# Late heads on SP's queue: a head's store and load of turned probabilities, then the loads of values, queries and keys

## The chip, the cores and the metric

The kernel runs on one core of a Trainium2 chip. The metric is the device time in microseconds (us) of one launch, the median of several runs.

## The reference

Causal attention with a forget gate (4 batches of 8 heads, 576 positions, head size 64) is followed by two dense layers with different activations. Cut to what is computed:

```python
scores = scale * np.matmul(q, k.transpose(0, 1, 3, 2))
cum = np.cumsum(np.log(np.clip(f, 0.0001, 1.0)), axis=-1)
scores = np.where(causal, -1e9, scores + cum[..., :, None] - cum[..., None, :])
attn = np.exp(scores - max); attn = attn / (sum + 1e-09)
x = np.matmul(attn, v)                      # 2304 tokens x 512
h = np.maximum(x @ w_in, 0.0);  x = (h * h) @ w_out        # first layer, d_ff 2048
h = x @ w_in2;                  y = (h - np.tanh(h)) @ w_out2   # second layer
```

## The kernel before

The 32 heads go through attention one by one, while TensorE also works on the first dense layer for tokens whose attention is ready (blocks of 288 tokens, matmuls into hp and yp, L143 and L169). Heads 0 to 15 transpose their probabilities on TensorE. Heads 16 to 31, the late heads, do it in another way, and the change touches these alone:

- scores(k): five tiles of queries, t = 4, 3, 2, 1, 0. TensorE multiplies QA and QB (L490, L491), DVE takes the row minimum out of PSUM into a tile T (L451), ScalarE takes the exponential (L456), and DVE (t = 4, 2, 0) or POOL (t = 3, 1) normalises (L465).
- turn(k, t): DVE transposes each tile in T by blocks of 32 x 32 (L517).
- put_get(k): SP issues five stores of T to a buffer in HBM (p_d, L526 and L527), and after they have landed six loads back into T with the blocks exchanged (L532 and L534).
- split_p(k): POOL makes the high part PTh from T (L95, four instructions), DVE the low part PTl (L106, four).
- pv(k): TensorE multiplies PTh and PTl with the values (o_ps, L576, L570, L573). For an odd head a store of the result follows (x_d, L440 and L441).

There are two tiles T, one for even and one for odd heads (T_191 and T_192 in the rows of the instruction order). PTh and PTl exist once. A head's inputs come by load(u), which fetches queries and keys into R (576 KB, one buffer) and the gate's rows into QB (18 KB, two buffers), and load_v(u), which fetches values into VR (160 KB, two buffers). prep(u) makes QA and QB out of R on ScalarE, DVE and POOL. All these DMAs are issued by SP, in the order of its queue: an instruction that waits holds all that stand behind it.

attention_late() writes the steps of head k and of head k - 1 in turns, in five pieces for each k. From the third block of the dense layer on, which holds nearly all of the late heads, the order on each engine is not the order of this code. A scheduler makes it at build time from the dependencies and its own estimates, so an added tie can move instructions on every engine.

Of the kernel before, what the change touches and what calls it, by code (L numbers as in the profile page):

```python
# [18 lines left out]
NU = B * H  # L19
# [14 lines left out]
UT = 16  # L34
# [24 lines left out]
def kernel(  # L59
# [25 lines left out]
    def pre(u):  # L85
        return "" if u < UT else "l_"

    def by(name):
        return {"A": nc.scalar, "V": nc.vector, "P": nc.gpsimd, "S": nc.sync}[ENG[name]]

    def rounded(eng, out, in_):
        if eng is nc.scalar:
            eng.activation(out, in_, AF.Copy)  # L93
        elif eng is nc.gpsimd:
            eng.tensor_scalar(out, in_, 1.0, 1.0, ALU.mult, ALU.mult)  # L95
        else:
            eng.tensor_copy(out, in_)
# [85 lines left out]
    def latest(engine):  # L183
        return next(x for x in reversed(nc.cur_bb.bb.instructions) if x.engine == engine)
# [43 lines left out]
    def load(u):  # L228
        R[u] = one.tile([128, 2, S], F32, tag="R", name="R")
        nc.sync.dma_start(R[u], qk[u])  # L230
        QB[u] = two.tile([68, 2, S], F32R, tag="QB", name="QB")
        nc.sync.dma_start(QB[u][64:68].bitcast(F32), aug_d[u])
# [15 lines left out]
    def load_v(u):  # L248
        VR[u] = two.tile([128, 5, D], F32, tag="VR", bufs=2, name="VR")
        nc.sync.dma_start(VR[u], v[u])  # L250
# [183 lines left out]
    def store_x(b, pair, xs, c0, c1):  # L434
        STORED.add((b, pair, c1))
        n = c1 - c0
        xh = one.tile([128, S], F32R, tag="xsh", name="xsh")
        rounded(by(pre(b * H) + "xh"), xh[:, :n], xs[:, c0:c1])
        rest(by(pre(b * H) + "xl"), xs[:, c0:c1], xs[:, c0:c1], xh[:, :n])
        nc.sync.dma_start(x_d[b][pair][:, 0, c0:c1], xh[:, :n].bitcast(F32))  # L440
        nc.sync.dma_start(x_d[b][pair][:, 1, c0:c1], xs[:, c0:c1])  # L441
# [25 lines left out]
    def bank(u, name):  # L467
        return psa.tile([128, 512], F32, tag="at", name=name)

    def blocks(u):  # L470
        return PT[u % 2].rearrange("p (k s j) -> p k s j", s=4, j=32)
# [10 lines left out]
    def scores(u, t):  # L482
        qa, qb, st = QA[u], QB[u], ST[u]
        n, q0 = NKEY[t], Q0[t]
        rows = 64 if t == 0 else 128
        cuts = [(0, 320), (320, 576)] if t == 4 else [(0, n)]
        mn = None
        for i, (a, b) in enumerate(cuts):
            ps = bank(u, "s_ps")
            nc.tensor.matmul(ps[:, :b - a], qa[:, 0, q0:q0 + 128], qa[:, 1, a:b], start=True, stop=False)  # L490
            nc.tensor.matmul(ps[:, :b - a], qb[:, 0, q0:q0 + 128], qb[:, 1, a:b], start=False, stop=True)  # L491
            mn = row_min(prob(u, t, a, b), ps, st, t, i, a, b, mn)
        soften(prob(u, t, 0, n), st, t, mn, f"{pre(u)}n{t}")
# [29 lines left out]
    def put_get(u):  # L523
        T, (d, e) = PT[u % 2], p_d[u % 2]
        for q in range(4):
            by("put").dma_start(d.rearrange("(i q) n -> q i n", q=4)[q], T[32 * q:32 * q + 32, :2048])  # L526
        by("put").dma_start(e, T[:, 2048:])  # L527
        src = d.rearrange("(i q) (a b n) -> b i (q a) n", q=4, a=4, b=4)
        end = e.rearrange("(q i) (b s n) -> b i q s n", q=4, b=2, s=2)
        for b in range(4):  # L530
            dst = T[32 * b:32 * b + 32]
            by("get").dma_start(dst[:, :2048].rearrange("p (q n) -> p q n", q=16), src[b])  # L532
            if b < 2:
                by("get").dma_start(dst[:, 2048:].rearrange("p (q n) -> p q n", q=4), end[b][:, :, 1])  # L534
# [9 lines left out]
    def late_pt(k):  # L544
        return PT[k].rearrange("p c j -> p (c j)")[:, :1664].rearrange("p (q c j) -> p q c j", q=4, j=32)

    def pv(u):
        vh, vr = VH.pop(u), VR.pop(u)
        b, h = divmod(u, H)
        e = h % 2  # L550
        ps = bank(u, "o_ps")
        if u < UT:
            hi, lo = (PT[k] for k in "hl")
            po = ps.rearrange("p (s j) -> p s j", s=4)
            at = lambda p, c, t: p[:, 10 - 4 * c + t:14 - 4 * c]
            po4, p4 = ps[0:64, 384:512].rearrange("p (q j) -> p q j", q=4), blocks(0)[0:64, 12:16, 1]
            po_at = lambda t: po[:, t:]
            p0 = blocks(0)[0:64, 8:10, 0]
        else:
            hi, lo = (late_pt(k) for k in "hl")  # L560
            po = ps.rearrange("p (q s j) -> p q s j", q=4, s=4)
            at = lambda p, c, t: p[:, :, CHUNK_AT[c]:CHUNK_AT[c] + 4 - t]
            end = PT[u % 2][0:64, 2048:].rearrange("p (q s j) -> p q s j", q=4, s=2)
            po4, p4 = po[0:64, :, 3], end[:, :, 1]
            po_at = lambda t: po[:, :, t:]
            p0 = end[:, 0:2, 0]
        seq = [(hi, 0), (None, 4), (None, 0), (hi, 1), (lo, 1), (hi, 2), (lo, 2), (hi, 3), (lo, 3), (lo, 0)]
        for n, (pt, c) in enumerate(seq):
            if c == 4:
                nc.tensor.matmul(po4, vr[0:64, 4], p4, start=False, stop=False)  # L570
            elif pt is None:
                ps0 = bank(u, "o0_ps")
                nc.tensor.matmul(ps0[0:64, 0:64], vr[0:64, 0], p0, start=True, stop=True)  # L573
            else:
                t = max(0, c - 1)
                nc.tensor.matmul(po_at(t), vh[:, c].rearrange("p a d -> p (a d)"), at(pt, c, t), start=(n == 0), stop=(n == 9))  # L576
        if e == 0:
            XS[0] = two.tile([128, S], F32, tag="xs", name="xs")
        xs = XS[0]
        r = slice(64 * e, 64 * e + 64)  # L580
        xt = one.tile([64, 512], F32, tag="xsh", name="xt")
        rounded(nc.scalar, xt, ps[64:128])
        if u < UT:
            nc.vector.tensor_tensor(xs[r, 64:], ps[0:64], xt, ALU.add)
        else:
            nc.vector.tensor_tensor(
                xs[r, 64:].rearrange("p (s q j) -> p q s j", s=4, q=4),
                ps[0:64].rearrange("p (q s j) -> p q s j", q=4, s=4),
                xt.rearrange("p (q s j) -> p q s j", q=4, s=4), ALU.add,
            )  # L590
        rounded(by(pre(u) + "xs0"), xs[r, 0:64], ps0[0:64, 0:64])
        if e == 1:
            store_x(b, h // 2, xs, 0, S)
# [11 lines left out]
    def attention(u0):  # L605
        for p in range(u0 - 2, UT):
            if u0 - 1 <= p:
                load_v(p + 1)
            for t in (1, 4, 3, 2):
                if p >= u0:  # L610
                    trans(p, t)
                    yield
                if u0 <= p + 1:
                    scores(p + 1, t)
                    if t == 1:
                        scores(p + 1, 0)
                    elif p + 1 == UT:
                        turn(UT, t)
                    yield
                if t == 4 and p + 2 < NU:  # L620
                    prep(p + 2)
                if t == 3 and p >= u0:
                    prep_v(p)
            if p + 3 < NU:
                load(p + 3)
            if p >= u0:
                pv(p)
            if p + 1 == UT:
                turn(UT, 1)
                turn(UT, 0)  # L630
                put_get(UT)
            if p >= u0:
                yield

    def attention_late():
        for k in range(UT + 1, NU + 1):
            now = k < NU
            if now:
                load_v(k)
                clear(k)  # L640
                scores(k, 4)
            yield
            if now:
                scores(k, 3)
                turn(k, 4)
            yield
            if k + 1 < NU:
                prep(k + 1)
            prep_v(k - 1)
            split_p(k - 1, 0)  # L650
            if now:
                scores(k, 2)
                turn(k, 3)
            yield
            if k + 2 < NU:
                load(k + 2)
            split_p(k - 1, 1)
            if now:
                scores(k, 1)
                scores(k, 0)  # L660
                turn(k, 2)
            yield
            if now:
                turn(k, 1)
                turn(k, 0)
                put_get(k)
            pv(k - 1)
            yield

    X = {0: [f1.tile([128, NK, TB], F32R, tag="xhl", bufs=4, name="xhl") for _ in range(2)]}  # L670
# [223 lines left out]
```

## Time and profile before

| | |
|---|---|
| median of 3 runs | 1102.18 us (1101.27 to 1104.58) |
| profiled execution | 1104.67 us, span 1102.8 us |
| PE busy | 1032.4 us, 94% of the span |
| DVE, ACT, POOL busy | 585.9, 526.7, 255.0 us |
| mean granted TensorE clock | 0.97 |

The share of PE is an average over stages: after some 575 us the attention is over and PE is busy all the time, so the stretch ahead of that is where an order of transfers could matter.

### The profile page before, as it was taken

What the parts mean: (1) busy time and instruction counts of PE and PEld (TensorE: products, weight loads), DVE (VectorE), ACT (ScalarE), POOL (GpSimd) and SP (SyncE); (2) the same over time, 40 slices, a digit from 0 to 9 for tenths busy, and PEclk for the clock granted to TensorE, in tenths of its full rate; (3) what the DMA queues carried; (4) which work ended last, traced back from release to release, by engine and by line L of the source; (5) the groups of instructions that cost most, each with busy time, mean ns of one, the idle gap of its engine ahead of it and who ended that gap; (6) DMA issues with size and microseconds to landing.
All of it is one profiled execution on the core that took longest, in us unless ns stands there. A gap on an engine that the chain in (4) does not pass through costs nothing.

```text
span 1102.8 us, 17026 instructions
## 1 busy us (share of the span) xinstructions
PE 1032.4 (94%) x6048; PEld 909.0 (82%) x6048; DVE 585.9 (53%) x1550; ACT 526.7 (48%) x1221; POOL 255.0 (23%) x374
## 2 busy tenths in 40 slices
PE   4899999998989789989799999999999999999998
PEld 3576779887978688879789999888888888888898
DVE  5886777776677666957533545644222222222222
ACT  6977777764554454645435757532222222222222
POOL 4244455555345353533310000000000000000000
PEclk9989999998998898999899999999999999999999
DMA  7556643228766758766738149300300200110010
GB/s 243 193 148 196 183 154 121 79 79 234 213 172 181 208 146 257 222 145 176 197 84 328 53 143 345 133 1 1 115 1 1 88 27 1 39 39 1 1 39 20
DMA packets 95558, 137.99 MB, mean 125 GB/s; under 512 B 12048, under 2 KB 72016, under 8 KB 93424
## 3 DMA queue, kind: packets, MB, share of 16 engines
q1 hardware_dynamic: 95472, 136.89, 41.4%
q8 instruction: 48, 0.79, 0.3%
q14 instruction: 38, 0.31, 0.1%
HBM read 94.99 MB, written 41.88 MB: 124 GB/s over the span
## 4 chain that ended last, share of the span: by engine, by line
PE 51%; DMA 9%; DVE 4%; SPq 4%; POOL 1%; issue 1%; ACT 1%; POOLq 0%; ACTq 0%; DVEq 0%
PE yp L169 25%; PE hp L143 24%; DMA p_d<-T 4%; DMA T<-p_d 3%; DVE PTl L106 1%; SPq L532 1%; SPq L526 1%; PE o_ps L576 1%; SPq L534 1%; POOL PTh L95 1%; DMA xhl<-x_d 1%; DMA raw<-in_w_dram 1%; DVE T L517 1%; DVE gl L106 1%; DVE T L465 0%
## 5 line engine op out<-in xcount | busy, mean ns | idle before, releaser
L143 PE MATMUL hp<-xhl,w 128*128 128x288 f32 (+2 forms) x2496 | 457.5, 331 | 6.7 <-ACT tmp L153 4.0
L143 PEld LDWEIGHTS hp<-xhl,w 128*128 128x128 f32 x2496 | 394.6, 194 | 45.5 <-ACT tmp L153 5.2
L169 PE MATMUL yp<-ghl,w 128*128 128x512 f32 (+1 forms) x960 | 214.9, 373 | 0.0
L169 PE MATMUL yp<-gh,w 128*128 128x288 f32 x1024 | 199.3, 301 | 0.0
L169 PEld LDWEIGHTS yp<-ghl,w 128*128 128x128 f32 x960 | 167.8, 188 | 34.2
L169 PEld LDWEIGHTS yp<-gh,w 128*128 128x128 f32 x1024 | 161.6, 192 | 1.6 <-issue 0.4
L158 DVE TENSOR_TENSOR tmp<-hp,tmp 128x512 f32<-128x512 f32 (+1 forms) x80 | 51.0, 638 | 208.2 <-ACT tmp L157 208.1
L157 ACT ACTIVATE tmp<-hp 128x512 f32<-128x512 f32 (+1 forms) x80 | 44.5, 556 | 223.2 <-PE hp L143 223.1
L169 PE MATMUL yp<-gl,w 128*128 128x288 f32 x512 | 132.7, 303 | 4.6 <-DVE gl L106 3.7
L153 ACT ACTIVATE tmp<-hp 128x288 f32<-128x288 f32 x128 | 51.7, 405 | 123.3 <-PE hp L143 121.7
L456 ACT ACTIVATE T<-T,ST 128x320 f32<-128x320 f32 (+4 forms) x152 | 82.8, 546 | 45.8 <-DVE ST L451 39.4
L169 PEld LDWEIGHTS yp<-gl,w 128*128 128x128 f32 x512 | 91.0, 193 | 7.2 <-DVE gl L106 5.1
L106 DVE TENSOR_TENSOR gl<-tmp,gh 128x288 fp32r<-128x288 f32 x96 | 47.8, 499 | 64.5 <-ACT tmp L155 63.9
L106 DVE TENSOR_TENSOR PTl<-T,PTh 128x512 fp32r<-128x512 f32 (+1 forms) x64 | 53.0, 857 | 50.0 <-POOL PTh L95 49.0
L106 DVE TENSOR_TENSOR ghl<-tmp,ghl 128x512 fp32r<-128x512 f32 (+1 forms) x80 | 51.1, 639 | 49.1 <-ACT ghl L93 43.8
L451 DVE CUSTOM_DVE_ANT_0 T<-s_ps,mk 128x320 f32<-128x320 f32 (+3 forms) x152 | 61.8, 421 | 21.4 <-PE s_ps L491 13.2
L465 POOL TENSOR_SCALAR T<-T,ST 128x448 f32<-128x448 f32 (+4 forms) x80 | 52.4, 657 | 89.6 <-DVE ST L460 43.3
L93 ACT ACTIVATE ghl<-tmp 128x512 fp32r<-128x512 f32 (+1 forms) x80 | 47.2, 590 | 49.9 <-DVE tmp L158 49.8
L576 PE MATMUL o_ps<-PTh,VH 128*128 128x512 f32 (+1 forms) x96 | 40.4, 421 | 29.3 <-POOL PTh L95 25.4
L95 POOL TENSOR_SCALAR PTh<-T 128x512 fp32r<-128x512 f32 (+1 forms) x64 | 43.9, 710 | 73.3 <-DMA T<-p_d 72.8
L106 DVE TENSOR_TENSOR w<-wst,w 128x512 fp32r<-128x512 f32 x64 | 45.8, 722 | 25.8 <-ACT w L93 25.6
L154 ACT ACTIVATE gh<-tmp 128x288 fp32r<-128x288 f32 x128 | 56.6, 443 | 4.4 <-PE yp L169 1.3
(119 smaller groups left out, 1217.3 us busy)
## 6 DMA issues: line engine op xcount, KB each, us to landing
raw<-in_w_dram SPq DMA_DIRECT2D x64, 512.0 KB
p_d<-T SPq DMA_DIRECT2D x64, 256.0 KB
T<-p_d SPq DMA_DIRECT2D x64, 256.0 KB
R<-in_qk_dram SPq DMA_DIRECT2D x24, 576.0 KB
xhl<-y_d SPq DMA_DIRECT2D x16, 512.0 KB
xhl<-x_d SPq DMA_DIRECT2D x14, 576.0 KB
y_d<-yst SPq DMA_DIRECT2D x14, 576.0 KB
VR<-in_v_dram SPq DMA_DIRECT2D x32, 160.0 KB
```

Source lines behind the costliest of these rows:

```text
L93: eng.activation(out, in_, AF.Copy)
L95: eng.tensor_scalar(out, in_, 1.0, 1.0, ALU.mult, ALU.mult)
L106: eng.tensor_tensor(out, in_, hi.bitcast(F32), ALU.subtract)
L143: nc.tensor.matmul(ps, w[:, k * 128:(k + 1) * 128], xk, start=(jj == 0), stop=(jj == 11))
L153: nc.scalar.activation(tmp, ps, AF.Relu)
L154: nc.scalar.activation(gh, tmp, AF.Square)
L158: nc.vector.tensor_tensor(tmp, ps, tmp, ALU.subtract)
L169: nc.tensor.matmul(yp[m][:, :n], w[:, c], x, start=(i == 0 and j == 0), stop=(i == NF - 1 and j == 2))
L451: nc.vector.tensor_tensor_reduce(out, s_in, m_in, -0.125, 3.0e38 if mn is None else mn, ALU.add, ALU.min, accum_out=acc)
L456: nc.scalar.activation(p, p, AF.Exp, bias=mn, scale=-1.0, accum_out=st[:rows, 1, t:t + 1])
L465: by(n_by).tensor_scalar(p, p, st[:rows, 3, t:t + 1], 1.0, ALU.mult, ALU.mult)
L576: nc.tensor.matmul(po_at(t), vh[:, c].rearrange("p a d -> p (a d)"), at(pt, c, t), start=(n == 0), stop=(n == 9))
```

## The change

The loads of values, queries and keys no longer stand in the pieces of attention_late() where they are first allowed. A new function loads(k) issues them at the end of head k's last piece, and ties each of them behind the last SP instruction traced so far. Head k now calls for the values of head k + 1 and the queries and keys of head k + 2. The load that the earlier loop made for the last two heads of its own is left out there, and loads(16) makes it.

```diff
-            if p + 3 < NU:
+            if p + 3 < NU and p + 1 < UT:
                 load(p + 3)
...
                 put_get(UT)
+                loads(UT)
...
+    def loads(k):
+
+        with tc.issue_after(latest(EngineType.SP)):
+            if k + 1 < NU:
+                load_v(k + 1)
+            if k + 2 < NU:
+                load(k + 2)
...
             if now:
-                load_v(k)
                 clear(k)
...
-            if k + 2 < NU:
-                load(k + 2)
             split_p(k - 1, 1)
...
             pv(k - 1)
+            loads(k)
             yield
```

On SP's queue, between the loads back of head 18 (even) and those of head 19 (odd), before the change:

```order
L440 DMA x_d_69<-xsh 128x576
L441 DMA x_d_69<-xs 128x576
L232 DMA QB<-aug_d 4x1152
L250 DMA VR<-in_v_dram 128x320
L230 DMA R<-in_qk_dram 128x1152
L526 DMA p_d_73<-T_192 32x2048 x4
L527 DMA p_d_74<-T_192 128x256
L532 DMA T_192<-p_d_73 32x16x128
```

And with the change, from head 19's store to head 20's:

```order
L526 DMA p_d_73<-T_192 32x2048 x4
L527 DMA p_d_74<-T_192 128x256
L532 DMA T_192<-p_d_73 32x16x128
L534 DMA T_192<-p_d_74 32x4x64
L532 DMA T_192<-p_d_73 32x16x128
L534 DMA T_192<-p_d_74 32x4x64
L532 DMA T_192<-p_d_73 32x16x128 x2
L250 DMA VR<-in_v_dram 128x320
L230 DMA R<-in_qk_dram 128x1152
L232 DMA QB<-aug_d 4x1152
```

The load of R that stood ahead of head 19's store was that of head 22. Now the one behind its loads back is that of head 21, so queries and keys come one head later against the stores.

On POOL, around head 19's split (PTh from T_192) and head 20's two normalisations (L465 on T_191), before:

```order
L465 TENSOR_SCALAR T_191<-T_191,ST 128x14x32
L95 TENSOR_SCALAR QB<-QA 64x576
L106 TENSOR_TENSOR QB<-R,QA 64x576
L465 TENSOR_SCALAR T_191<-T_191,ST 128x6x32
L95 TENSOR_SCALAR PTh<-T_192 128x4x128 x2
L95 TENSOR_SCALAR PTh<-T_192 128x4x96
L95 TENSOR_SCALAR PTh<-T_192 128x4x64
```

And with the change:

```order
L95 TENSOR_SCALAR PTh<-T_192 128x4x128 x2
L95 TENSOR_SCALAR PTh<-T_192 128x4x96
L95 TENSOR_SCALAR PTh<-T_192 128x4x64
L465 TENSOR_SCALAR T_191<-T_191,ST 128x14x32
L521 MEMSET T_192 128x3x2x32
L95 TENSOR_SCALAR QB<-QA 64x576
L106 TENSOR_TENSOR QB<-R,QA 64x576
L465 TENSOR_SCALAR T_191<-T_191,ST 128x6x32
```

Head 20's normalisations stood ahead of head 19's split, which waits for head 19's loads back. They now stand behind it. For head 21 it is the other way round: both its normalisations stood behind head 20's split, and now both stand ahead of it. On POOL around the splits of heads 28 and 29, with the change:

```order
L95 TENSOR_SCALAR PTh<-T_191 128x4x64
L465 TENSOR_SCALAR T_192<-T_192,ST 128x14x32
L465 TENSOR_SCALAR T_192<-T_192,ST 128x6x32
...
L465 TENSOR_SCALAR T_191<-T_191,ST 128x14x32
L95 TENSOR_SCALAR PTh<-T_192 128x4x128 x2
L95 TENSOR_SCALAR PTh<-T_192 128x4x96
L95 TENSOR_SCALAR PTh<-T_192 128x4x64
...
L465 TENSOR_SCALAR T_191<-T_191,ST 128x6x32
```

Here head 30's second normalisation stands behind head 29's split; before the change both stood ahead of it.

## Rows read from the trace of the kernel before

**Rows 1.** Busy time by stretch: engines, granted clock, share of DMA, GB/s
```profile
271.76:569.14 297.38, 262.45 (x1716) 248.16 (x1716) 197.82 (x592) 147.68 (x375) 117.71 (x161) 0.92 0.70 190
569.14:1102.80 533.66, 528.53 (x2860) 460.64 (x2860) 187.26 (x324) 184.92 (x362) 4.11 (x5) 1.00 0.20 71
```

**Rows 2.** Timeline of POOL, the splits alone: start, us, idle before and its releaser
```profile
271.76 2.48 POOL L95 TENSOR_SCALAR PTh<-T 128x512 fp32r<-128x512 f32 x4 [6.99 <-DMA T<-p_d]
...
291.44 2.31 POOL L95 TENSOR_SCALAR PTh<-T 128x512 fp32r<-128x512 f32 x4
...
310.21 2.68 POOL L95 TENSOR_SCALAR PTh<-T 128x512 fp32r<-128x512 f32 x4 [5.18 <-DMA T<-p_d]
...
332.36 2.91 POOL L95 TENSOR_SCALAR PTh<-T 128x512 fp32r<-128x512 f32 x4 [5.04 <-DMA T<-p_d]
...
344.76 3.13 POOL L95 TENSOR_SCALAR PTh<-T 128x512 fp32r<-128x512 f32 x4
...
369.29 2.91 POOL L95 TENSOR_SCALAR PTh<-T 128x512 fp32r<-128x512 f32 x4 [9.43 <-DMA T<-p_d]
...
391.64 2.91 POOL L95 TENSOR_SCALAR PTh<-T 128x512 fp32r<-128x512 f32 x4 [0.54 <-issue]
...
403.63 2.47 POOL L95 TENSOR_SCALAR PTh<-T 128x512 fp32r<-128x512 f32 x4 [8.03 <-DMA T<-p_d]
...
430.57 2.91 POOL L95 TENSOR_SCALAR PTh<-T 128x512 fp32r<-128x512 f32 x4 [3.69 <-DMA T<-p_d]
...
445.92 2.98 POOL L95 TENSOR_SCALAR PTh<-T 128x512 fp32r<-128x512 f32 x4 [1.10 <-DMA T<-p_d]
...
474.87 2.92 POOL L95 TENSOR_SCALAR PTh<-T 128x512 fp32r<-128x512 f32 x4 [8.40 <-DMA T<-p_d]
...
487.23 2.48 POOL L95 TENSOR_SCALAR PTh<-T 128x512 fp32r<-128x512 f32 x4 [3.92 <-DMA T<-p_d]
...
510.81 2.92 POOL L95 TENSOR_SCALAR PTh<-T 128x512 fp32r<-128x512 f32 x4 [3.21 <-DMA T<-p_d]
...
531.95 2.68 POOL L95 TENSOR_SCALAR PTh<-T 128x512 fp32r<-128x512 f32 x4 [5.54 <-DMA T<-p_d]
...
545.60 2.49 POOL L95 TENSOR_SCALAR PTh<-T 128x512 fp32r<-128x512 f32 x4 [0.52 <-DMA T<-p_d]
...
569.14 2.68 POOL L95 TENSOR_SCALAR PTh<-T 128x512 fp32r<-128x512 f32 x4 [11.74 <-DMA T<-p_d]
```

**Rows 3.** Waits between 255 and 580 us: total, times, longest
```profile
POOL PTh L95 <- DMA T<-p_d: 72.8, 13, 11.7
```

**Rows 4.** Timeline of DVE near head 19's last turns
```profile
318.23 0.24 DVE L517 STREAM_TRANSPOSE T<-T 64x64 f32<-64x64 f32 x1
```

**Rows 5.** Timeline of SP: heads 19 and 29, store and first load back
```profile
315.66 0.33 SPq L230 DMA_DIRECT2D R<-in_qk_dram  x1
318.09 2.69 SPq L526 DMA_DIRECT2D p_d<-T  x4
320.88 1.07 SPq L527 DMA_DIRECT2D p_d<-T  x1
324.66 0.54 SPq L532 DMA_DIRECT2D T<-p_d  x1
...
327.17 1.21 SPq L532 DMA_DIRECT2D T<-p_d  x2
...
518.17 2.67 SPq L526 DMA_DIRECT2D p_d<-T  x4
520.94 1.07 SPq L527 DMA_DIRECT2D p_d<-T  x1
524.58 0.55 SPq L532 DMA_DIRECT2D T<-p_d  x1
```

**Rows 6.** Chain that ended last: one load of queries and keys, issue to landing
```profile
451.69 3.56 DMA R<-in_qk_dram
```

**Rows 7.** Timeline of ScalarE: first step of prep
```profile
258.82 1.17 ACT L93 ACTIVATE QA<-R 128x1152 fp32r<-128x1152 f32 x1 [0.71 <-PE s_ps L490]
```

## The prediction, made before the changed kernel was run

> **What bounds the kernel now.** I read the busy time by stretch first. Once the last late head is split, from 569 us on, PE is busy 528.5 of 533.7 us at full clock: nothing that SP issues can shorten that. In the stretch from the first to the last split of a late head, 297.4 us for 15 heads, PE is busy 262.5 us and its granted clock is 0.92 [rows 1]. The change touches this stretch alone, so it can win at most what PE lacks there: 34.9 us of idle time, and some 0.08 x 297 = 24 us of clock.
>
> What PE lacks it for, the waits tell: POOL sat 72.8 us in front of the split PTh until a head's loads back from HBM had landed [rows 3], and pv stands behind the split. So I took the 16 splits as mile posts. Row n of the timeline of POOL is head 15 + n, and the distance of two rows is one step [rows 2]. The 15 steps, heads 17 to 31, are 19.7, 18.8, 22.2, 12.4, 24.5, 22.4, 12.0, 26.9, 15.4, 29.0, 12.4, 23.6, 21.1, 13.7, 23.5 us, together 297.4. The reader is to see two kinds, around 13 and around 23 us. The instruction order explains them. A late head's two normalisations on POOL, and the turns on DVE behind them, stand either all **ahead** of the previous head's split (heads 17, 20, 23, 25, 27 and 30) or some of them **behind** it (18, 19, 21, 22, 24, 26, 28, 29, 31). If they are behind, the head can't be stored before its predecessor has come back, and two round trips through HBM follow one another. If they are ahead, the two overlap.
>
> One behind step, read in full: head 18 is split at 310.2; head 19's last turn starts at 318.2 [rows 4]; SP's first store of head 19 starts at 318.1, the last store at 320.9, the first load back at 324.7, the last ones at 327.2 [rows 5]; the split of head 19 is at 332.4 [rows 2]. That is 8 us until the last turn and 14 us of round trip.
>
> **The change, part by part.**
>
> *What SP sends first.* The edit is meant for a queue on which loads hold a store up. In the case above they don't: head 19's store starts with the last turn (318.1 against 318.2) though a load of R stood ahead of it [rows 4, 5]. Nor does R's traffic hold the store up on the way: from the issue of head 19's last store to the first load back it is 3.78 us, with R issued 2.4 us ahead of the store; for head 29, whose load of R is long past, 3.64 us [rows 5]. The difference is 0.14 us; for each of the 14 late loads of R (heads 18 to 31) that is 2 us at most, and with half the heads not waiting for their store I put it at nothing. Its bounds: no gain below, and above the rest of R's 3.56 us [rows 6] that is still under way at the store, 1.1 us for head 19 and 16 us for 14 like it.
>
> The Trainium skill (DMA: Bandwidth & Descriptors, Queues, rings and completion order) says that each DMA engine takes descriptors in ring order, so that R's 576 KB would have to go ahead of the store. By that rule the change would give those 16 us back, and by the two rows 2 us; the rows decide, and I keep the rule's result as a rival below.
>
> *Loads behind the loads back.* R for head k + 2 now leaves after head k's loads back, and SP can go on to them at once. For head 19 the last loads back stop issuing at 328.4. Had R followed at some 329, it would land at 332.6 by its 3.56 us [rows 5, 6], about when POOL starts the split of 2.9 us [rows 2]. ScalarE's first step of prep takes 1.2 us [rows 7] and would end ahead of the split's end at 335.3, so POOL's part of prep behind the split finds its data. The split covers it: 0 us. If R had to wait until the loads back are through, it would land at 335.9, prep's part for POOL could start at 337.1, and 1.8 us would be added. In the new order that part follows directly on the split for about six heads, so the upper bound is 11 us.
>
> *What the tie does to the other engines.* This is the term that I expect to count. The scheduler has moved instructions on POOL and DVE. I went through both orders head by head with the same question. With the change, ahead are heads 17, 21, 23, 25 and 27; behind are 18, 19, 20, 22, 24, 26, 28, 29, 30 and 31. So heads 20 and 30 have gone behind, and head 21 has come ahead. From the steps of before: the nine behind make 212.0 us, 23.55 each; of the ahead ones head 17 is 19.7, which the change doesn't touch (its loads back run beside two 576 KB loads of x), and the other five make 65.8, 13.15 each [rows 2].
>
> Sum with the change: 10 x 23.55 + 19.7 + 4 x 13.15 = 307.8 us against 297.4, or **10.4 us more**, one step of the one kind turned into the other. PE pays it as idle time, since the dense layer's matmuls behind pv wait in line. The bounds of this term: the shortest behind step against the longest ahead one is 18.8 - 15.4 = 3.4 us, the other way 29.0 - 12.0 = 17.0 us [rows 2]. I take the means, because both kinds were drawn from all over the stretch.
>
> No instruction is added or removed on any computing engine, and PE's work after the last split is the same, so nothing else enters. The profiled execution took 1104.67 us, 2.5 above the median of 1102.18; 1104.7 + 10.4 = 1115.1, and against the median **1112.6**, rounded to 1113.
>
> **The rivals.**
>
> *Shorter behind steps: faster.* The ten behind steps need not keep their mean, since what stands between split and last turn has been reshuffled too. Break-even is (297.4 - 19.7 - 52.6) / 10 = 22.5 us for each, only 1.05 below the mean. For it: heads 18 and 29 show 18.8 and 21.1 us, and for heads 19, 29, 30 and 31 the new order leaves only about three of the five turns behind the split. Against it: heads 22, 24 and 28 have some scores as well as their turns behind it. If all ten fall to head 29's 21.14, the sum is 283.7, a gain of 13.7 us, and the median 1088.5. It decides from 22.5 us on.
>
> *R out of the way: no change.* If every store did queue behind R, 16 us come back against the 10.4 lost, 1097; with the nine behind heads alone gaining, 9 x 1.1 = 10 us, it ends at nothing, 1102, which I take. The 0.14 us speaks against it. The Trainium skill's rule above speaks for it.
>
> *R late: slower still.* The 11 us of the second part come on top of the 10.4: 1123.6. For it: the single buffer of R is now filled one head later than before, so a reserve of a whole step has gone. Against: the split of 2.9 us covers most of it.
>
> **How the numbers follow.** I call 0.3%, 3.3 us, the least that a measurement of this kernel tells from no change. The forecast, slower by 3 to 17 us (1105 to 1119), gets 0.48; R late, up to 1124 and a little beyond, 0.12; no change 0.13; shorter behind steps 0.27. Slower is then 0.60, same 0.13, faster 0.27. The range leaves out the far tails of both: it reaches down to the gain of 13.7 (1088) and up to 1125.
>
> **What would show it.** In the profile of the changed kernel the 16 splits should again stand in steps of two kinds, short for heads 21, 23, 25 and 27, long for 20 and 30, with some 308 us from the first to the last. POOL's wait for the loads back should grow beyond 72.8 us, and PE's busy time after the last split stay at some 528 us. The gap from a head's last store to its first load back should stay at 3.6 to 3.8 us. The prediction is wrong if long steps stand below 22.5 us in the mean, if the two kinds are no longer to be seen, or if POOL waits for R (through QA) rather than for the loads back.

## The result, and the profile after

The changed kernel took 1115.31 us (median of 4 runs, 1110.57 to 1115.97) against 1103.21 us before on the same chip: a ratio of 1.0102, 95% interval 1.0069 to 1.0135. It is 12 us slower. The profiled execution has a span of 1113.4 us.

The busy time by stretch, cut at the first and the last split of a late head as in [rows 1]. The columns are the stretch, its length, the busy time of TensorE, of its weight loads, of DVE, ScalarE and POOL (with the number of instructions), the granted clock, the share of DMA and GB/s:

```profile
271.04:580.47 309.43, 269.06 (x1720) 253.15 (x1720) 201.45 (x595) 150.03 (x377) 121.68 (x165) 0.90 0.69 187
580.47:1113.40 532.93, 528.34 (x2856) 460.91 (x2856) 186.88 (x323) 184.87 (x362) 4.34 (x5) 0.99 0.20 71
```

The whole loss lies in the first row: 309.4 us where it was 297.4. PE's idle time there is 40.4 us (34.9 before), and its busy time is 6.6 us longer at a granted clock of 0.90 (0.92 before). After the last split the two kernels are within 1 us of each other.

The 16 splits on POOL, from its timeline, as in [rows 2]:

```profile
271.04 2.48 POOL L95 TENSOR_SCALAR PTh<-T 128x512 fp32r<-128x512 f32 x4 [7.91 <-DMA T<-p_d]
285.31 2.25 POOL L95 TENSOR_SCALAR PTh<-T 128x512 fp32r<-128x512 f32 x4
306.62 2.54 POOL L95 TENSOR_SCALAR PTh<-T 128x512 fp32r<-128x512 f32 x4 [3.52 <-DMA T<-p_d]
325.47 2.91 POOL L95 TENSOR_SCALAR PTh<-T 128x512 fp32r<-128x512 f32 x4 [10.87 <-DMA T<-p_d]
348.63 2.92 POOL L95 TENSOR_SCALAR PTh<-T 128x512 fp32r<-128x512 f32 x4 [4.78 <-DMA T<-p_d]
362.99 2.47 POOL L95 TENSOR_SCALAR PTh<-T 128x512 fp32r<-128x512 f32 x4 [6.30 <-DMA T<-p_d]
390.79 2.91 POOL L95 TENSOR_SCALAR PTh<-T 128x512 fp32r<-128x512 f32 x4 [4.04 <-DMA T<-p_d]
403.59 2.92 POOL L95 TENSOR_SCALAR PTh<-T 128x512 fp32r<-128x512 f32 x4 [3.13 <-DMA T<-p_d]
434.71 3.00 POOL L95 TENSOR_SCALAR PTh<-T 128x512 fp32r<-128x512 f32 x4
448.93 2.97 POOL L95 TENSOR_SCALAR PTh<-T 128x512 fp32r<-128x512 f32 x4 [3.49 <-DMA T<-p_d]
478.70 2.91 POOL L95 TENSOR_SCALAR PTh<-T 128x512 fp32r<-128x512 f32 x4 [1.04 <-DMA T<-p_d]
489.40 2.48 POOL L95 TENSOR_SCALAR PTh<-T 128x512 fp32r<-128x512 f32 x4 [6.73 <-DMA T<-p_d]
518.45 2.91 POOL L95 TENSOR_SCALAR PTh<-T 128x512 fp32r<-128x512 f32 x4 [7.54 <-DMA VR<-in_v_dram]
538.86 2.68 POOL L95 TENSOR_SCALAR PTh<-T 128x512 fp32r<-128x512 f32 x4 [4.82 <-DMA T<-p_d]
561.99 2.92 POOL L95 TENSOR_SCALAR PTh<-T 128x512 fp32r<-128x512 f32 x4 [3.88 <-DMA T<-p_d]
580.47 2.90 POOL L95 TENSOR_SCALAR PTh<-T 128x512 fp32r<-128x512 f32 x4 [8.72 <-DMA T<-p_d]
```

The steps of heads 17 to 31 are 14.3, 21.3, 18.9, 23.2, 14.4, 27.8, 12.8, 31.1, 14.2, 29.8, 10.7, 29.1, 20.4, 23.1 and 18.5 us. The two kinds are there: heads 21, 23, 25 and 27, ahead, have 13.0 us in the mean, the ten behind heads 24.3 us. Heads 20 and 30 have become long (12.4 and 13.7 before), head 21 short (24.5 before).

The waits between 255 and 592 us (engine and tile, released by; total us, times, longest), cut 12 us later than [rows 3] since the last split is later:

```profile
POOL PTh L95 <- DMA T<-p_d: 69.2, 13, 10.9
...
ACT QA L93 <- DMA R<-in_qk_dram: 49.6, 13, 6.8
...
POOL QB L95 <- ACT QA L93: 13.0, 7, 5.6
```

POOL's wait for the loads back has hardly grown beyond the 72.8 us of before. Head 28's wait of 7.5 us stands in the list above under VR, but the split reads T and no values; at the same place a second profile of the change names T<-p_d. With it the sum is 76.7 us, and 74.5 in the second profile. What is new is that the first step of prep, on ScalarE, waits 13 times for queries and keys to land, where none of its waits in this window was for them before, and that POOL waits 13.0 us for that step (5.8 before).

Head 19's last turn on DVE, its store and loads back and the load of R behind them on SP, and ScalarE's first step of prep on that R, from their timelines, as in [rows 4, 5]:

```profile
312.44 0.24 DVE L517 STREAM_TRANSPOSE T<-T 64x64 f32<-64x64 f32 x1
```

```profile
314.16 1.07 SPq L527 DMA_DIRECT2D p_d<-T  x1
317.88 0.56 SPq L532 DMA_DIRECT2D T<-p_d  x1
...
320.39 1.22 SPq L532 DMA_DIRECT2D T<-p_d  x2
321.65 0.61 SPq L250 DMA_DIRECT2D VR<-in_v_dram  x1
322.36 0.38 SPq L230 DMA_DIRECT2D R<-in_qk_dram  x1
```

```profile
327.64 1.17 ACT L93 ACTIVATE QA<-R 128x1152 fp32r<-128x1152 f32 x1 [5.45 <-DMA R<-in_qk_dram]
```

From the last store's issue to the first load back it is 3.72 us, as before. The split follows at 325.5, 3.9 us after the last load back is issued (321.6): a split that waits for nothing else stands there. R is issued at 322.36, and ScalarE, which waits for it, starts at 327.64: some 5.3 us to land. Over the 13 places where ScalarE waits for R that time is 5.0 to 8.9 us, 6.3 in the median.

At head 24 something else holds it. First a piece of the chain that ended last, then ScalarE's and POOL's timelines, answering to [rows 6, 7]:

```profile
421.63 8.91 DMA R<-in_qk_dram
```

```profile
430.57 1.16 ACT L93 ACTIVATE QA<-R 128x1152 fp32r<-128x1152 f32 x1 [5.77 <-DMA R<-in_qk_dram]
```

```profile
431.82 1.23 POOL L95 TENSOR_SCALAR QB<-QA 64x576 fp32r<-64x576 f32 x1 [5.55 <-ACT QA L93]
433.02 1.60 POOL L106 TENSOR_TENSOR QB<-R,QA 64x576 fp32r<-64x576 f32 x1
```

R needs 8.91 us to land here, prep starts 8.94 us after R was issued, and the split of head 24, at 434.71, stands right behind prep's two instructions on POOL. This R, head 26's, stands in front of head 24's loads back, not behind them. The last SP instruction traced before loads(24) is the store of head 23's result (x_d), so the tie is to that, and the scheduler put it ahead of the loads back; at head 26 it is the same, for the other late heads R is behind. Head 24's last loads back were issued by 427.2, so by the 3.9 us of head 19 it could have started at some 431.1 (an estimate from these rows); its own row names no wait. This is the wait "for R (through QA)" that the prediction named as a sign against it.

### The profile page after: what moved, and what is told of

It reads as the page before. It is cut to its first block, busy times and chain, and to the rows that moved or that the text cites. A ratio compares the mean times of both kernels' runs of the same rounds, so it can differ in the third digit from the quotient of the medians.

```text
span 1113.4 us, 16991 instructions
## 1 busy us (share of the span) xinstructions
PE 1036.5 (93%) x6048; PEld 912.0 (82%) x6048; DVE 587.2 (53%) x1550; ACT 527.8 (47%) x1221; POOL 253.4 (23%) x374
## 4 chain that ended last, share of the span: by engine, by line
PE 64%; DMA 14%; DVE 9%; SPq 6%; ACT 4%; issue 2%; POOL 1%; POOLq 0%; ACTq 0%; DVEq 0%
PE hp L143 28%; PE yp L169 27%; DMA p_d<-T 6%; DMA T<-p_d 5%; SPq L532 2%; DVE PTl L106 2%; PE o_ps L576 2%; DMA R<-in_qk_dram 2%; PE o_ps L372 2%; SPq L526 2%; DMA raw<-in_w_dram 1%; SPq L534 1%; DVE T L451 1%; ACT T L456 1%; PE s_ps L490 1%
## 5 line engine op out<-in xcount | busy, mean ns | idle before, releaser
L169 PE MATMUL yp<-gh,w 128*128 128x288 f32 x1024 | 202.7, 303 | 3.0 <-ACT gh L154 1.5
L456 ACT ACTIVATE T<-T,ST 128x320 f32<-128x320 f32 (+4 forms) x152 | 83.1, 547 | 60.0 <-DVE ST L451 49.6
L106 DVE TENSOR_TENSOR gl<-tmp,gh 128x288 fp32r<-128x288 f32 x96 | 52.2, 546 | 62.1 <-ACT tmp L155 61.4
L451 DVE CUSTOM_DVE_ANT_0 T<-s_ps,mk 128x320 f32<-128x320 f32 (+3 forms) x152 | 62.3, 423 | 28.3 <-PE s_ps L491 17.7
L465 POOL TENSOR_SCALAR T<-T,ST 128x448 f32<-128x448 f32 (+4 forms) x80 | 52.2, 655 | 106.4 <-DVE ST L460 49.7
L106 DVE TENSOR_TENSOR PTl<-T,PTh 128x512 fp32r<-128x512 f32 (+1 forms) x64 | 49.3, 794 | 50.2 <-POOL PTh L95 50.1
L576 PE MATMUL o_ps<-PTh,VH 128*128 128x512 f32 (+1 forms) x96 | 41.0, 427 | 27.8 <-POOL PTh L95 25.1
L93 ACT ACTIVATE QA<-R 128x1152 fp32r<-128x1152 f32 (+1 forms) x32 | 33.7, 1054 | 55.6 <-DMA R<-in_qk_dram 55.1
```

What stands on the lines that cost most here:

```text
L106: eng.tensor_tensor(out, in_, hi.bitcast(F32), ALU.subtract)
L169: nc.tensor.matmul(yp[m][:, :n], w[:, c], x, start=(i == 0 and j == 0), stop=(i == NF - 1 and j == 2))
L451: nc.vector.tensor_tensor_reduce(out, s_in, m_in, -0.125, 3.0e38 if mn is None else mn, ALU.add, ALU.min, accum_out=acc)
L456: nc.scalar.activation(p, p, AF.Exp, bias=mn, scale=-1.0, accum_out=st[:rows, 1, t:t + 1])
L465: by(n_by).tensor_scalar(p, p, st[:rows, 3, t:t + 1], 1.0, ALU.mult, ALU.mult)
```

## The experiments

Lines in these kernels lie some lines lower than in the kernel before; the tiles name the work. Where a kernel keeps the order of another one, its instructions on PE, DVE, ScalarE and POOL are tied one behind the other in that order, and only SP's differ. The diffs here are cut to what a run changes, with switches written out and names shortened:

```diff
+    like = build(True, names(build(False, [], "tied")), "tied")
+    placed, forced = names(like), {}
+    for engine, emitted in EMITTED.items():
+        if not engine.endswith("SP"):
+            at = {name: n for n, name in enumerate(emitted)}
+            forced[engine] = [at[name] for name in placed if name in at]
+    nc = build(True, names(build(False, [])), "soon", forced)
```

Ratios are to the kernel before, timed beside each run at 1105.1 to 1105.7 us. The last column is from one profiled execution each:

| run | us | ratio, 95% interval | first to last split, us |
|---|---|---|---|
| queries and keys sooner, changed order | 1122.05 | 1.0148 (1.0119 to 1.0178) | 312.2 |
| the same again | 1124.19 | 1.0171 (1.0144 to 1.0199) | 314.8 |
| the change again, beside it | 1114.40 | 1.0094 (1.0066 to 1.0122) | 304.3 |
| values tied, order of before | 1106.21 | 1.0007 (0.9994 to 1.0019) | 298.0 |
| values tied, own order | 1113.19 | 1.0081 (1.0063 to 1.0098) | 294.7 |
| queries and keys tied, own order | 1117.24 | 1.0111 (1.0088 to 1.0133) | 309.0 |
| change, splits 19 and 29 later | 1119.69 | 1.0123 (1.0101 to 1.0144) | 313.9 |
| before, splits 19 and 29 sooner | 1123.75 | 1.0162 (1.0143 to 1.0181) | 318.1 |
| all heads ahead, early loads | 1063.36 | 0.9617 (0.9589 to 0.9646) | 255.8 |
| all heads ahead, tied loads | 1094.96 | 0.9901 (0.9878 to 0.9924) | 294.3 |
| the last one with queries and keys sooner | 1063.06 | 0.9616 (0.9589 to 0.9642) | 263.5 |
| all heads ahead, early, values tied | 1065.33 | 0.9640 (0.9615 to 0.9665) | 256.9 |

**Queries and keys sooner, in the order of the changed kernel.** From head 17 on, R and QB are loaded where the kernel before called for them, as soon as their buffers are free; the values stay tied.

```diff
+            if k + 2 < NU:
+                load(k + 2)
             split_p(k - 1, 1)
...
             if k + 1 < NU:
                 load_v(k + 1)
-            if k + 2 < NU:
+            if k + 2 < NU and k == UT:
                 load(k + 2)
```

> Engines other than SP run exactly the changed kernel's order; from head 17 on, R and QB are loaded as soon as their buffers are free, not behind the loads back. Theory of order (two kinds of steps; heads 20 and 30 behind their predecessor's split): the 16 splits keep their steps, about 309 us from first to last, and the time stays at 1112 to 1116 us. Rival, R late: ScalarE's 49.6 us of waiting for R in the changed kernel is what costs; the wait falls below 10 us and the time to 1101 to 1107 us.

It was slower than the change, not faster, though ScalarE's wait for R fell from 49.6 to 3.8 us. The intervals of the two overlapped, so both were timed again on one chip:

> The changed kernel as it stands, timed again beside the run with queries and keys loaded sooner in the same order of the other engines. Both theories: 1.007 to 1.014 times the kernel before.

> As the first run of this kernel: the order of every engine but SP is that of the changed kernel, queries and keys are loaded as soon as their buffers are free. If loads behind the loads back help by themselves, this run is slower than the changed kernel by some 5 us, ratio 1.0119 to 1.0178; if the two first runs differed by chance of the chip, both are within 2 us of each other.

1114.40 against 1124.19 us: with the other engines' order held, queries and keys loaded late are worth 9.8 us (by the first two ratios 5). So the order alone, with loads as soon as they may go, costs 16 to 19 us over the kernel before, more than the change as a whole. The steps show how. Heads 20, 21 and 30, which the order flips, change by +10.8, -10.2 and +9.5 us in the change, 10.1 together, and by 11.9 and 11.4 together in the two profiles with loads sooner. What the stretch loses beyond that with loads sooner (14.8 and 17.4 us in all) lies in heads that kept their kind.

POOL's waits show both sides of the late loads. For loads back it waits 88.2 and 93.1 us with loads sooner, against 76.7 and 74.5 in the change; for prep 0.3 and 0.5 us against 13.0 and 12.4. One place where time is won can be read. Head 18 with loads sooner, DVE, SP and POOL:

```profile
303.45 0.24 DVE L522 STREAM_TRANSPOSE T<-T 64x64 f32<-64x64 f32 x1
```

```profile
302.52 0.80 SPq L531 DMA_DIRECT2D p_d<-T  x2
303.48 0.46 SPq L235 DMA_DIRECT2D R<-in_qk_dram  x1
303.99 1.71 SPq L531 DMA_DIRECT2D p_d<-T  x2
305.80 0.58 SPq L532 DMA_DIRECT2D p_d<-T  x1
...
310.33 0.56 SPq L537 DMA_DIRECT2D T<-p_d  x1
```

```profile
318.46 2.54 POOL L100 TENSOR_SCALAR PTh<-T 128x512 fp32r<-128x512 f32 x4 [6.71 <-DMA T<-p_d]
```

The same head in the changed kernel, DVE and SP; its split is in the list above, at 306.62:

```profile
294.35 0.24 DVE L517 STREAM_TRANSPOSE T<-T 64x64 f32<-64x64 f32 x1
```

```profile
292.51 2.69 SPq L526 DMA_DIRECT2D p_d<-T  x4
295.30 1.07 SPq L527 DMA_DIRECT2D p_d<-T  x1
...
299.07 0.56 SPq L532 DMA_DIRECT2D T<-p_d  x1
```

From the first store's issue to the last one's it is 3.28 us with R among the stores and 2.79 without, the 0.5 us that SP spends on R. From there to the first load back it is 4.53 and 3.77 us, and from the first store to the split 15.9 and 14.1 us; the other profile of either kernel gives the same within 0.2 us. So head 18 wins 1.8 us. Not all of the 0.8 us on the way need be R's: the second half of x_d and the values were also sent in between. Head 17, too, wins: its step is 14.3 and 14.9 us in the change, 16.4 and 18.8 with loads sooner.

The rest of the 9.8 us is not settled. Between the profiles of the two later runs the steps of heads 17 and 18 differ by 6.6 us, the other thirteen together by 3.9 us, and 4.4 us lie ahead of the first split. The two profiles with loads sooner are of one kernel, and the time ahead of the first split differs by 7.9 us between them (269.2 and 277.0), so that part shows nothing.

**Only the values tied, in the order of before.**

```diff
     with tc.issue_after(latest(EngineType.SP)):
         if k + 1 < NU:
             load_v(k + 1)
-        if k + 2 < NU:
-            load(k + 2)
```

> Engines other than SP run exactly the order of the kernel before; only the loads of values are tied behind the loads back on SP. Theory of order: nothing moves on the engines, so 1103 us, within 3 us, and nine heads behind as before. Rival, SP's queue (loads in front of a store cost, or loads behind it come late): a change of 5 us or more in either direction.

No change: 160 KB of values cost nothing that the run can tell in either place. Nor does holding the other engines' order by ties add any time that shows.

**The same, with the order that the scheduler makes of it.**

> Only the loads of values are moved and tied, and the scheduler orders anew. In its order only heads 17, 24 and 27 are ahead of their predecessor's split on POOL and DVE, 12 are behind. Theory of order: 19.7 + 12 x 23.55 + 2 x 13.15 = 328.6 us from first to last split against 297.4, so about 1134 us, 1119 to 1140. Rival, R late: R is loaded early here, so no slower than before, 1098 to 1106 us.

It is 0.8% slower, by the order alone. The stretch is shorter than before, 294.7 us, but 542.3 us are left after it (533.7 before): 68 matmuls of the dense layer that stood inside the stretch have gone behind it. Counting heads does not see that, and its 1134 us was far off.

**Only queries and keys tied, own order.** The loads of values stay where they were (the other half of the edit).

> Only the loads of queries and keys are moved and tied, and the scheduler orders anew. In its order heads 17, 21, 23, 25, 27, 29 and 31 are ahead, 8 are behind. Theory of order: 19.7 + 8 x 23.55 + 6 x 13.15 = 287.0 us from first to last split, 10 less than before, so about 1092 us, 1086 to 1100. Rival, R late: R is as late as in the changed kernel, so slower than before, 1108 to 1118 us.

The run is 1.1% slower than before. Beside head 17 six heads are ahead here, with 13.2 us in the mean, but the eight behind have 26.9, and ScalarE waits 58.5 us for R. Counting heads at 23.55 us fails again, this time because the run is slower than counted.

**Splits of heads 19 and 29 sooner, in the kernel before.** Only the order on POOL and DVE is changed (on SP, whose order is not held, one load of values and one store of yst move a few places): both splits go ahead of the rest of head 20's and head 30's normalisations and turns.

```diff
+    for u, n in ((19, 0), (29, 1)):
+        first = [x for x in mine if x in (turns[u + 1][1:] if "DVE" in engine else norms[u + 1][n:])]
+        i = mine.index(first[0])
+        soon = [x for x in mine[i:] if x in split[u]]
+        mine = mine[:i] + soon + [x for x in mine[i:] if x not in soon]
```

> The kernel before, its loads where they were, but on POOL and DVE the splits of heads 19 and 29 come ahead of what is left of the normalisations and turns of heads 20 and 30: these two heads are behind, as with the change, and nothing else moves. Theory 1 (a flip from ahead to behind lengthens one step by some 10 us): 6 to 11 us slower, up to 1110 to 1114, heads 20 and 30 at some 20 to 23 us. Theory 2 (the loop of one buffer T bounds two steps together): heads 20 and 30 longer, heads 21 and 31 shorter by as much, no change within 4 us, 1101 to 1108.

It is 18.0 us slower. The splits of heads 19, 20, 29 and 30 on POOL:

```profile
331.68 2.91 POOL L107 TENSOR_SCALAR PTh<-T 128x512 fp32r<-128x512 f32 x4 [11.46 <-DMA T<-p_d]
354.33 2.91 POOL L107 TENSOR_SCALAR PTh<-T 128x512 fp32r<-128x512 f32 x4 [4.17 <-DMA T<-p_d]
...
540.86 2.90 POOL L107 TENSOR_SCALAR PTh<-T 128x512 fp32r<-128x512 f32 x4 [12.71 <-DMA T<-p_d]
566.71 2.91 POOL L107 TENSOR_SCALAR PTh<-T 128x512 fp32r<-128x512 f32 x4 [5.21 <-DMA T<-p_d]
```

Heads 20 and 30 take 22.7 and 25.9 us instead of 12.4 and 13.7, and heads 21 and 31 give nothing back (25.1 and 22.6 against 24.5 and 23.5). The stretch is 20.7 us longer, or 10.4 for each flip (9.0 by the medians). Where loads are early, the price of a flip is what the prediction made it; the loop over one buffer T as a bound on pairs falls.

**Splits of heads 19 and 29 later, in the changed kernel.** The reverse edit, under the tied loads: the two splits move behind the normalisations and turns of heads 20 and 30. SP's order is not held, so it is not quite that of the change: three stores of results and one load of values come some places later.

> Everything as in the changed kernel, SP's queue too, but on POOL and DVE the splits of heads 19 and 29 come after the normalisations and turns of heads 20 and 30, so that these two heads are ahead again as they were before the change. Theory 1 (each flip from behind to ahead shortens one step from some 23 to 13 us): heads 20 and 30 take some 13 us, about 8 us come back for each less what their successors give back; 6 to 11 us in all, first to last split some 300 us, 1104 to 1109 us. Theory 2 (two steps together are bound by the loop of one buffer T, so that a short step makes the next one longer): heads 20 and 30 become short, heads 21 and 31 long, no change within 4 us, 1111 to 1119.

Nothing is won: a ratio of 1.0123 where the change has 1.0102 and 1.0094. Heads 20 and 30 do get shorter (17.7 and 20.1 us), but heads 19 and 29 get longer by more (25.6 and 28.1, after 18.9 and 20.4). SP and POOL around head 19's split:

```profile
323.50 0.38 SPq L242 DMA_DIRECT2D R<-in_qk_dram  x1
```

```profile
330.05 1.24 POOL L107 TENSOR_SCALAR QB<-QA 64x576 fp32r<-64x576 f32 x1 [7.24 <-ACT QA L105]
...
333.03 2.90 POOL L107 TENSOR_SCALAR PTh<-T 128x512 fp32r<-128x512 f32 x4
```

The reason is R. Head 21's queries and keys leave behind head 19's loads back, POOL waits 7.24 us for head 21's prep, and the split now stands behind that prep. It comes 10.3 us after the last loads back were issued (322.7), where 3.9 us do. At head 29 it is the same: POOL waits 9.05 us for prep, and the split follows 3.1 us after that prep starts. This is neither of the two theories stated ahead of the run: not one buffer T, but the late R, undoes the flip.

**All heads ahead.** If that is so, all heads ahead must be fast with early loads and slow with tied ones. In both kernels the split of head k - 1 is written and tied behind head k's last turn:

```diff
-            split_p(k - 1, 0)
...
-            split_p(k - 1, 1)
...
                 put_get(k)
+                with tc.issue_after(latest(EngineType.DVE)), tc.issue_after(latest(EngineType.Pool)):
+                    split_p(k - 1, 0)
+                    split_p(k - 1, 1)
             pv(k - 1)
```

> The loads of the kernel before, but the split of head k - 1 is written and tied behind the last turn of head k on DVE and POOL for all late heads, so that every head from 17 on is ahead. Theory 1 (an ahead step costs 13 us whatever stands before it): the bound is then PE, 262 us of work in the stretch, so first to last split 262 to 275 us, 1068 to 1085. Theory 2 (two steps together can't go below what one buffer T needs from split to split, 35 to 45 us in the traces so far): steps of 18 to 22 us each without two kinds, first to last split 280 to 310 us, 1087 to 1115.

> The changed kernel with every head from 17 on ahead, by the same tie as in the run with the early loads. Theory 1: first to last split 262 to 275 us, 1068 to 1085 us. Theory 2: 280 to 310 us, 1087 to 1115. If the place of the loads counts by itself, this run and the one with the early loads, both with all heads ahead, differ by more than 4 us: by what the loads behind give (faster here) if stores were held up by R, slower here if R comes late for prep.

With the loads of before: 1063.36 us, 42 us faster than before. The stretch from first to last split by busy time:

```profile
276.90:532.70 255.80, 246.53 (x1720) 236.58 (x1720) 201.25 (x593) 145.79 (x375) 118.29 (x160) 0.98 0.81 220
```

The steps are 14.4 to 20.6 us, all of one kind. Against [rows 1], PE's idle time fell from 34.9 to 9.3 us and its busy time by 15.9 us at a granted clock of 0.98 (0.92 before), for 1720 and 1716 matmul records; the two make the 41.6 us. Steps cannot come down to 13 us each, since PE is now nearly full.

With the tied loads: 1094.96 us, 31.6 us of the gain are lost. Its waits between 255 and 592 us, and SP and POOL around head 25's split:

```profile
ACT QA L99 <- DMA R<-in_qk_dram: 54.3, 13, 7.0
POOL QB L101 <- ACT QA L99: 47.4, 12, 9.7
```

```profile
442.60 0.38 SPq L236 DMA_DIRECT2D R<-in_qk_dram  x1
```

```profile
449.73 1.24 POOL L101 TENSOR_SCALAR QB<-QA 64x576 fp32r<-64x576 f32 x1 [6.29 <-ACT QA L99]
...
453.71 2.90 POOL L101 TENSOR_SCALAR PTh<-T 128x512 fp32r<-128x512 f32 x4
```

It is the picture of head 19 with the splits later. Head 25's last loads back were issued by 441.8, R for head 27 behind them; POOL waits for head 27's prep, and the split comes 11.9 us after the loads back.

The two kernels' orders differ, so one of the two had to be held. The next run has every engine but SP in the order of the tied kernel, and loads R and QB sooner, by the same diff as above:

> All heads ahead; the order of every engine but SP is exactly that of the run with all heads ahead and tied loads, but from head 17 on queries and keys are loaded as soon as their buffers are free. Theory R late (with all heads ahead there is no longer a wait for loads back that covers the late R): ScalarE's 54 us of waits for R go, most of the 31 us between the two runs with all heads ahead comes back, 1063 to 1075 us. Theory order (the schedule made with tied loads is the worse one by itself): no change, 1090 to 1098.

It took 1063.06 us, 31.9 us less, or 31.5 by the two ratios, which were taken on different chips: all of the gain comes back. The same two places on POOL, the first of which no longer waits:

```profile
424.82 1.17 POOL L101 TENSOR_SCALAR QB<-QA 64x576 fp32r<-64x576 f32 x1
...
428.75 2.91 POOL L101 TENSOR_SCALAR PTh<-T 128x512 fp32r<-128x512 f32 x4
```

So the place of the loads of queries and keys alone, in an order in which heads are ahead, costs some 32 us.

> All heads ahead; the order of every engine but SP is exactly that of the run with all heads ahead and the early loads, only the values are loaded late and tied behind the loads back. As in the order of the kernel before, values come early enough either way: no change within 3 us of 1063. If a load of values ahead of a store holds it up: faster by up to 15 times the 0.8 us that 160 KB take at R's rate, 12 us.

1065.33 us, an interval that overlaps that of the early loads: values again count for nothing that the runs can tell. The 0.8 us in the text above is not R's rate as measured: 160 of 576 KB in 5.0 to 8.9 us make 1.4 to 2.5 us, which leaves the run's answer as it is.

## Why the prediction was right, and where it was not

- **The time.** Forecast 1113 (1105 to 1119 for the likeliest case), measured 1115.3. The steps were forecast at 307.8 us in all and are 309.4, in a second profile of the change 304.3.
- **What the tie does to the other engines: right, with its price shown.** The lists of heads ahead and behind came out as read from the order, and the three heads that changed their kind give 10.1 us in the change (10.8 in its second profile), where the sum has 10.4. Two flips in the kernel before cost 20.7 us, 10.4 each. That the tie reorders all engines is the cause of the loss: held in the order of before, tied values cost nothing, and the changed order costs 16 to 19 us with sooner loads. What the sum missed is the 3 to 6 us of the stretch that this order costs in heads which kept their kind: it let them keep their mean.
- **"PE pays it as idle time": about half.** Of the 12.0 us that the stretch is longer, 5.4 are idle time and 6.6 longer busy time at a granted clock of 0.90 instead of 0.92; in the second profile it is 4.2 and 2.7 us of 6.9, at 0.93.
- **"The change doesn't touch" head 17: wrong.** Its step shrank from 19.7 to 14.3 us. Before, head 17's split stood right behind prep's instructions on POOL, which had waited 2.1 us for QA and taken 2.7; that was head 20's prep, and in the new order no prep stands right ahead of this split (head 18's is at 273.8, head 19's behind the split). The order gives only part of it: in the same order with loads sooner the step is 16.4 and 18.8 us, and the split waits 2.7 and 3.9 us for loads back. The sum hid this, since the ten behind heads took 24.3 and not 23.55 us each, 7.6 in all.
- **What SP sends first, put at nothing: too low.** In one order of the other engines, late queries and keys are worth 5 to 10 us net of what a late R costs. One head 19 at 0.14 us was too thin a ground: at head 18 R in among the stores costs 0.5 us of SP's time and at most 0.8 us on the way. The Trainium skill's rule (DMA: Bandwidth & Descriptors, Queues, rings and completion order) that descriptors are taken in ring order points the right way, but the wait on the way is at most 0.8 us, not the whole of R's load.
- **Loads behind the loads back, put at nothing: wrong as a step.** It rested on R landing in 3.56 us, under a split's cover. That row of the chain [rows 6] was misread. The work behind it in the same chain is DVE's normalisation, which does not read R; ScalarE, which reads that R first, starts at 460.00, 8.3 us after the issue and without a wait for it:

```profile
455.31 0.21 DVE T L465
...
460.00 1.16 ACT QA L93
```

So 3.56 us is not shown to be a landing time. Where ScalarE waits for R, it takes 5.0 to 8.9 us; issued at 329 it would have landed at 335.3 by the median of 6.3, and the split's cover would have fallen short by 1.2 us (an estimate from these rows). Queries and keys also come two heads later, not one: the R behind head 19's loads back was head 23's before (329.0) and is head 21's now. At head 24 R took 8.91 us, and the split stood behind prep, where nothing covers it. POOL waits 13.0 us for prep in seven places. In this kernel the end of that is small, since with loads sooner POOL waits no less in all (88.2 and 93.1 us for loads back); it is some 32 us where all heads are ahead.

- **The signs.** POOL's wait for the loads back grew, but only from 72.8 to 76.7 us (74.5 in the second profile); the longer steps show up as waits of other kinds as well, and the wait for R through QA, named as a sign against the prediction, came with 13.0 us beside it. The others came as foretold: 3.72 us from store to load back, 528.3 us of PE behind the last split, long steps above 22.5 us.
- **The rivals.** Shorter behind steps fell: 24.3 us in the mean. R out of the way and R late are both real; together they give back 5 to 10 us, and the order's price is larger.

The two terms put at nothing were a gain of 5 to 10 us, and the order's whole price was 6 to 8 us above the 10.4: the mechanism was right, but that the sum came so near is in part luck, since errors cancelled. Not settled is where most of the gain of the late loads lies beyond heads 17 and 18. Built without the tie, the moved loads leave the other engines' order as it was, and on SP only one 18 KB load of QB changes its place, by two; that kernel was not run. Queries and keys tied in the order of before were not run either. Since a late load's worth depends on the order, the two shares, 16 to 19 us for the order and 5 to 10 back, hold for the order of the change alone.

## What to carry to other kernels

An added tie on one queue may matter less through that queue than through what the scheduler then does on every engine: compare the orders, price one flip, and hold the order of the rest when a load's place is to be judged. A load's landing time is read where its first reader waits for it, not from any piece of a chain. Whether a late load costs anything depends on what stands in order behind the work that needs it: the same late loads won 5 to 10 us in one order and lost some 32 in another. Here the better change was to let a head finish its turns ahead of its predecessor's split, with loads left early: 1063 us, 3.8% below the kernel before.

## What the runs showed of the hardware

- The same 576 KB load of R took 5.0 us (behind head 27's loads back) to 8.9 us (ahead of head 24's) to land in the 13 places of the changed kernel where ScalarE waited for it: a load's time read once is no price for it elsewhere.
- A store behind such a load on the same queue came back at most 0.8 us later (4.53 against 3.77 us at head 18), though R itself took 5.0 us or more wherever the changed kernel waited for it.
- The granted clock of the stretch was 0.90 with 40 us of PE idle time, 0.92 with 35 and 0.98 with 9; the second profile of the change has 0.93 with 39, so the idle time alone does not give it. Some 16 of the 41.6 us that all heads ahead won there came from the clock: 262.45 x 0.92 / 0.98 is 246.4, and PE's busy time was 246.53.
